# Block-causal attention with a top-1 MoE: x rows fetched four slots ahead, and the router of one batch laid beside its ranks

## Chip, core and metric

One Trainium2 chip, one core of it. The time is device microseconds (us) of one launch, from the first to the last instruction and what the launch has around it. Three runs of the kernel before gave 879.25, 882.23 and 882.85 us, so the median is 882.23 us.

The engines are named as in the profile: PE multiplies matrices (PEld loads its weights), DVE, ACT and POOL work on tiles, SP issues most of the loads. An engine executes its instructions strictly in the order in which they stand in its program. A name with q behind it (SPq) is the engine's own instruction queue: loads that it issues, branches, register loads.

## The reference

q, k, v are 8 batches x 8 heads x 576 tokens x 64. The attention is block-causal (blocks of 64 tokens); its output, 4608 tokens x 512, goes into a mixture of 8 experts of which each token takes one.

```python
scores = np.matmul(q, k.transpose(0, 1, 3, 2)) / 8
scores = np.where(pos[:, None] // 64 >= pos[None, :] // 64, scores, -1e9)
attn = softmax(scores)
x = np.matmul(attn, v).transpose(0, 2, 1, 3).reshape(4608, 512)

logits = normed(x) @ normed(expert_emb).T / tau        # 4608 x 8
expert = argmax(logits, axis=1)
gate = softmax(logits)[expert]
for e in range(8):
    m = expert == e
    out[m] = gate[m, None] * (relu(x[m] @ w1[e]) @ w2[e])   # 512 -> 1024 -> 512
```

## The kernel before, in words

**Attention (0 to about 341 us).** The work is cut in 32 pairs of heads, and each pair in pieces (scores, maxes, values and sums, finish) that a hand-written string orders. The router of a batch, `route(b)`, is a generator that gives one step at a time to places in those strings: the highest logit of a token, its expert, its rank among the tokens of that expert (`above`, `places`), the norm of its row (`squares`, then a power on POOL), the gate (`gx`, an exp on ACT), and at last five scatters (L654, an indirect DMA from POOL) that write the rows of x, with the gate and the token's number behind each row, into a DRAM buffer `xs` sorted by expert. Batch 6 (`b == B - 2`) is the last batch but one, and its router also decides which rows of two "early" tiles are valid (`einv`, `lack`).

**Early tiles (about 344 to 384 us).** Two tiles of 128 rows of expert 0 are calculated before the other tokens are sorted, with the chain that makes the tables of slots running beside them. Their rows are loaded by `early_rows` (`ex`, `eg`), and `place` makes from the token numbers the indices `ei` of the rows of the output.

**Slots (about 384 us to the end).** Up to 43 slots of 128 sorted rows, 36 of which run. Per slot: the first layer `ph` (PE, three products for each pair of tiles, since each fp32 operand is split in a high and a low part), relu on ACT to `h`, 16 transposes of `h` on DVE to `pt`, the split of `pt` into `hh` (ACT) and `hl` (DVE), the second layer `py` (PE), the scaling by the gate (ACT, `y`), the indirect store (POOL). `back(g)` writes down the engines' work in a fixed order; PE gets the second layer of slot g-1 behind the first layer of slot g. The rows of x are loaded into `xq` (four DMAs of 64 KB) and `gt` (gate and token) by `fetch(g)`, transposed on DVE to `px` (`xturn`), and split on ACT and POOL.

**Weights.** An expert has a ring half of `ring_h` and `ring_l` for each layer. At the first slot of an expert, ACT makes `ring_h` from `raw` (eight casts), POOL makes `ring_l = raw - ring_h` (eight subtractions), and SP loads the next expert's `raw` in four DMAs of 512 KB for each layer. "raw0" is the first layer's weights, "raw1" the second's. All this is conditional (`tc.If`, L1005 on SP) on a flag of the slot, read into registers on ACT, POOL and SP (`flags`, L968 and L969).

**SP's order.** In a steady slot SP has: the register loads of `flags`, the If of raw1, the If of raw0, `fetch` (a register load of the place, then `xq` x4 and `gt`), and so again. For 3 <= g < 8 `fetch` also has a `clear`: 260 KB of zeros written behind the last rows of an expert in `xs`, and the load of x waits for it to land. `fetch(3)` stands behind slot 0's `give_slot`.

Of the kernel before, what the change touches and what calls it, by code (L numbers as in the profile page):

```python
# [48 lines left out]
def kernel(  # L49
# [515 lines left out]
    def route(b, xrow, lgh, ssp):  # L565
# [3 lines left out]
        t1 = sm.tile([P, NJ, E], F32, name="t1")  # L569
        ohb, acc = hot[b % 2][:, 0:NJ, :], hot[b % 2][:, NJ, :]  # L570
        eng = nc.gpsimd if b < B - 1 else nc.vector
        nc.vector.tensor_reduce(lg, lgh.rearrange("p j h e -> p j e h"), axis=AX.X, op=ALU.add)
        yield
        nc.vector.tensor_reduce(mx, lg, axis=AX.X, op=ALU.max)
        yield
        eng.tensor_tensor(lg, lg, bc(mx.unsqueeze(2), P, NJ, E), op=ALU.subtract)
        yield

        nc.vector.scalar_tensor_tensor(t1, lg, 0.0, erev, op0=ALU.is_ge, op1=ALU.mult)
        yield  # L580
        nc.vector.tensor_reduce(mx, t1, axis=AX.X, op=ALU.max)
        yield
        nc.vector.tensor_tensor(ohb, t1, bc(mx.unsqueeze(2), P, NJ, E), op=ALU.is_equal)
        yield
        nc.vector.memset(ohb[64:P, NJ - 1, :], 0.0)
        yield
# [10 lines left out]
        if b < B - 1:  # L597
            t2 = above(rk)
            give_bank(rb)
        yield  # L600
        acc = hot[(b + 1) % 2][:, NJ, :]
        with nc.allow_low_precision(reason="whole numbers up to 42"):
            nc.vector.tensor_reduce(acc, hot[b % 2].rearrange("p j e -> p e j"), axis=AX.X, op=ALU.add)
        yield
# [6 lines left out]
        if b == B - 2:  # L611

# [6 lines left out]
            give_bank(cb)  # L619
            yield  # L620
            nc.vector.tensor_scalar(lack, miss, 0.0, float(EARLY), op0=ALU.max, op1=ALU.min)
            nc.gpsimd.tensor_scalar(einv, lim2, miss, BIG, op0=ALU.is_le, op1=ALU.mult)
            yield
            nc.vector.tensor_tensor(acc[:, 0:1], acc[:, 0:1], lack, op=ALU.add)
            yield

        ss = sm.tile([P, NJ], F32, name="ss")
        gs = sm.tile([P, NJ], F32, name="gs")
        if b < B - 1:
            for j in range(NJ):  # L630
                squares(xrow[:, j, 0:DM], ss[:, j:j + 1])
                yield
        else:
            nc.vector.tensor_reduce(ss, ssp, axis=AX.X, op=ALU.add)
        nc.gpsimd.tensor_tensor(ss, ss, half, op=ALU.pow)
        if b == B - 1:
            yield
        eng.tensor_scalar(ss, ss, 1.0e-6, None, op0=ALU.add)
        yield
        if b < B - 1:  # L640
            rowj = yield from places(t2, ohb, nc.gpsimd)
            yield
        nc.vector.reciprocal(ss, ss)
        yield
        eng.tensor_tensor(lg, lg, bc(ss.unsqueeze(2), P, NJ, E), op=ALU.mult)
        yield
        nc.scalar.activation(gx[b % 2][:, :, 0:E], lg, AF.Exp)
        yield
        nc.vector.tensor_reduce(gs, gx[b % 2], axis=AX.X, op=ALU.add)
        yield  # L650
        nc.vector.reciprocal(xrow[:, :, DM:DM + 1], gs.unsqueeze(2))
        yield
# [8 lines left out]
        if b == B - 2:  # L661
            slow.append(early_rows())
# [15 lines left out]
    def early_rows():  # L678
# [3 lines left out]
        for u in range(EARLY):  # L682
            place(ei[:, u:u + 1], eg[u], einv[:, u:u + 1])
# [177 lines left out]
    def counts():  # L861
# [26 lines left out]
        for e in range(AHEAD):  # L888
            clear(e)
        yield  # L890

# [48 lines left out]
    AHEAD = 3  # L940
    NFIRST = 5

# [65 lines left out]
    def fetch(g):  # L1008
        xq, gt = take("xq"), take("gt")
        if AHEAD <= g < E:  # L1010
            clear(g)
# [119 lines left out]
    def chain():  # L1131
# [18 lines left out]
        for u in range(60):  # L1150
            for w in list(work):
                try:
# [3 lines left out]
                    if w is tw:  # L1156
                        work.append(slot_places(0, NFIRST))
# [8 lines left out]
        for g in range(AHEAD):  # L1166
# [48 lines left out]
    rotate(mp, "gt", 5, [P, 2], F32)  # L1215
# [27 lines left out]
    def l2(g, parts):  # L1243
# [3 lines left out]
        if NF - 1 in parts:  # L1247
            u = g - NSLOT
# [209 lines left out]
```

## Time and profile before

| | |
|---|---|
| median of three runs | 882.23 us (879.25 to 882.85) |
| profiled execution, its own time | 879.04 us |
| its span, first to last instruction | 877.3 us |
| PE busy | 774.6 us (88% of the span) |
| DVE, POOL, ACT busy | 612.6, 461.1, 409.8 us |
| granted clock of PE, mean | 0.956 of full speed |
| 344.65 to 384.15, early tiles | PE busy 28.95 of 39.50 us |
| 384.15 to 455.58, slots 0 to 2 | PE busy 50.37 of 71.43 us |
| 455.58 to 655.92, slots on to the last stall | PE busy 155.67 of 200.34 us |
| 655.92 to the end | PE busy 209.81 of 221.41 us |

PE is the busiest engine; its idle time lies almost wholly between 341 and 656 us. A row of a timeline gives the start in us, the length, engine, line, operation, the tiles written and read, how many instructions are merged in the row, and in square brackets the engine's idle time just before it and what ended that idle time. "[11.02 <-ACT hh L1107]" says that the engine stood 11.02 us and went on when ACT had written hh in line 1107.

### The profile page before, as it was taken

What the parts mean: (1) busy time and instruction counts of PE and PEld (TensorE: products, weight loads), DVE (VectorE), ACT (ScalarE), POOL (GpSimd) and SP (SyncE); (2) the same over time, 40 slices, a digit from 0 to 9 for tenths busy, and PEclk for the clock granted to TensorE, in tenths of its full rate; (3) what the DMA queues carried; (4) which work ended last, traced back from release to release, by engine and by line L of the source; (5) the groups of instructions that cost most, each with busy time, mean ns of one, the idle gap of its engine ahead of it and who ended that gap; (6) DMA issues with size and microseconds to landing.
All of it is one profiled execution on the core that took longest, in us unless ns stands there. A gap on an engine that the chain in (4) does not pass through costs nothing. (4 is left out here: it accounts for less than half of the span.)

```text
span 877.3 us, 23684 instructions
## 1 busy us (share of the span) xinstructions
PE 774.6 (88%) x6989; PEld 619.4 (71%) x6989; DVE 612.6 (70%) x1363; ACT 409.8 (47%) x831; POOL 461.1 (53%) x462
## 2 busy tenths in 40 slices
PE   8999999999999997688489864968959999999994
PEld 3788878887888776466368653857838888888873
DVE  6577778777877775663778653747837888888870
ACT  2566666767676674354243361514423333443321
POOL 6556757686777765432534574646643222572221
PEclk9999999999999999899889978888979999999998
DMA  5645576563745403858254545454153111111110
GB/s 124 145 111 116 135 121 158 115 147 82 175 104 118 130 3 93 219 179 246 63 143 155 116 130 127 133 133 134 50 147 121 50 51 51 38 54 54 50 48 21
DMA packets 164234, 96.29 MB, mean 110 GB/s; under 512 B 125709, under 2 KB 146509, under 8 KB 164060
## 3 DMA queue, kind: packets, MB, share of 16 engines
q1 hardware_dynamic: 157084, 72.67, 35.6%
q0 software_dynamic: 6976, 21.66, 6.8%
q8 instruction: 65, 1.06, 0.5%
q14 instruction: 109, 0.89, 0.4%
HBM read 72.44 MB, written 23.27 MB: 109 GB/s over the span
## 5 line engine op out<-in xcount | busy, mean ns | idle before, releaser
L1101 DVE STREAM_TRANSPOSE pt<-h 32x256 f32<-32x256 f32 x528 | 240.7, 456 | 40.2 <-ACT h L1075 22.9
L1048 PE MATMUL py<-ring_h,hh 128*128 x272 | 113.7, 418 | 60.1 <-ACT hh L1107 60.0
L849 POOL TENSOR_TENSOR ring_l<-raw,ring_h 128x1024 f32 (+1 forms) x49 | 116.7, 2413 | 42.5 <-ACT ring_h L844 38.3
L361 DVE TENSOR_REDUCE nmx<-psm 128x16 f32<-128x1024 f32 (+2 forms) x128 | 125.6, 986 | 13.8 <-PE psm L355 10.9
L1048 PE MATMUL py<-ring_l,hh 128*128 x272 | 112.0, 412 | 0.0
L1048 PEld LDWEIGHTS py<-ring_h,hh 128*128 128x128 f32 x272 | 54.3, 200 | 75.9 <-ACT hh L1107 62.5
L844 ACT CAST ring_h<-raw 128x1024 f32 (+1 forms) x62 | 60.9, 1047 | 82.5 <-SPq L1005 63.8
L397 POOL TENSOR_TENSOR pS<-pS,pT 128x640 f32<-128x640 f32 (+2 forms) x93 | 93.5, 1006 | 9.8 <-ACT pT L423 4.1
L423 ACT ACTIVATE pT<-psm 128x640 f32<-128x640 f32 (+2 forms) x128 | 89.2, 703 | 18.5 <-PE psm L355 12.2
L1028 POOL TENSOR_TENSOR xl<-px,xh 128x512 fp32r<-128x512 f32 x34 | 43.8, 1289 | 98.3 <-ACT tb L958 75.4
L1048 PE MATMUL py<-ring_h,hl 128*128 x272 | 91.8, 400 | 0.0
L1048 PE MATMUL ph<-ring_h,xh 128*128 x280 | 87.4, 393 | 3.7 <-ACT y L1114 1.5
L1048 PE MATMUL ph<-ring_l,xh 128*128 x280 | 86.8, 391 | 0.4 <-POOLq L998 0.4
L1115 POOL DMA_INDIRECT out_dram<-y,oi x36 | 38.1, 1058 | 83.4 <-POOLq L998 34.9
L451 PE MATMUL psm<-pT,vo 128*64 128x320 f32 (+2 forms) x640 | 75.9, 380 | 0.0
L1114 ACT ACTIVATE y<-py,gt 128x512 f32<-128x512 f32 x34 | 23.4, 688 | 99.0 <-PE py L1048 97.1
L1048 PE MATMUL ph<-ring_h,xl 128*128 x280 | 69.1, 389 | 0.0
L416 PE MATMUL psm<-qh,kh 64*128 64x320 f32 (+4 forms) x384 | 66.8, 341 | 0.6 <-DVE ql L339 0.3
L1107 ACT CAST hh<-pt 128x512 fp32r<-128x512 f32 x66 | 35.5, 589 | 65.0 <-DVE pt L1101 63.9
L1048 PEld LDWEIGHTS ph<-ring_h,xh 128*128 128x128 f32 x280 | 52.3, 188 | 16.5 <-ACT y L1114 2.0
L1048 PEld LDWEIGHTS py<-ring_l,hh 128*128 128x128 f32 x272 | 54.3, 200 | 13.1
L451 PEld LDWEIGHTS psm<-pT,vo 128*64 128x64 f32 x640 | 43.2, 137 | 28.2 <-ACT pT L423 0.4
(260 smaller groups left out, 1674.1 us busy)
## 6 DMA issues: line engine op xcount, KB each, us to landing
raw<-in_moe_w_dram SPq DMA_DIRECT2D x60, 512.0 KB
xq<-xs SPq DMA_DIRECT2D x152, 64.0 KB
qn<-in_q_dram SPq DMA_DIRECT2D x64, 128.0 KB
kn<-in_k_dram SPq DMA_DIRECT2D x64, 128.0 KB
vo<-in_v_dram SPq DMA_DIRECT2D x64, 128.0 KB
xs<-zcol SPq DMA_DIRECT2D x8, 260.0 KB
raw<-in_moe_w_dram POOLq DMA_DIRECT2D x4, 512.0 KB, 4.6
qa<-nmT SPq DMA_DIRECT2D x64, 2.5 KB
```

What stands on the lines that cost most here:

```text
L361: nc.vector.tensor_reduce(m[:, :, f:f + o // w], mt[:, :, 0:o].rearrange("p h (b c) -> p h b c", c=w), axis=AX.X, op=ALU.max, negate=True)
L397: nc.gpsimd.tensor_tensor(o, o, pT[:, :, off[t]:off[t] + w], op=ALU.add)
L416: nc.tensor.matmul(st[0:kw, hh, o:o + c1 - c0], kk[hd[hh], t * P:t * P + kw], qq[hd[hh], 64 + c0:64 + c1], start=(x == 0), stop=(x == len( ...
L423: nc.scalar.activation(pT[:, :, f:f + w] if c0 else pA, st[:, :, 0:w], AF.Exp, scale=scale)
L451: m = nc.tensor.matmul(ob[hh * D:(hh + 1) * D, b0:b0 + q1 - c0], rows(vo, ends_v, n, t)[:, hh, :], pTs[hh][0][:, f0:f0 + q1 - c0] if c0 el ...
L844: return (nc.scalar.copy if eng is nc.scalar else eng.tensor_copy)(piece(ring_h, to, c, half), raw[i][:, c * CW:(c + 1) * CW])
L849: return eng.tensor_tensor(piece(ring_l, to, c, half), raw[i][:, c * CW:(c + 1) * CW], piece(ring_h, to, c, half).bitcast(F32), op=ALU.sub ...
L1028: eng.tensor_tensor(xl, slots[g]["px"].rearrange("p (c t) -> p c t", t=P), xh.bitcast(F32), op=ALU.subtract)
L1048: m = nc.tensor.matmul(out, ac, slots[g]["w", i](r, c * n + off), start=(u == 0 and c == 0), stop=(c == nk - 1 and u == len(turns) - 1))
L1101: nc.vector.transpose(pt[32 * j:32 * j + 32, :, 32 * i:32 * i + 32], h[32 * i:32 * i + 32, :, j, :])
L1107: nc.scalar.copy(sets["hh"][u], pt[:, 4 * u:4 * u + 4])
L1115: nc.gpsimd.indirect_dma_start(out=out, out_offset=bass.IndirectOffsetOnAxis(ap=to, axis=0), in_=y, in_offset=None, bounds_check=NT - 1, o ...
```

## The change

Three things are altered. First, `fetch` runs four slots ahead instead of three (`AHEAD`), and stands at the start of `back(g)`, not at its end. The three unconditional fetches and clears ahead of the slots stay three (`CLEAR`); `fetch(3)`, with its clear, goes between the loads of raw1 and raw0 in the early part, `fetch(4)` takes its old place, and `fetch(5)` is the first thing of `back(1)`. `gt` gets seven buffers. The tables' first piece covers eight slots (`NPLACE`) instead of five. Second, in `route(6)` the squares, the power and the gate are given out beside the rank's steps and not behind them, and `einv` and `lack` are made after the scatters. Third, the indices `ei` are made in `l2`, at the end of an early tile, and no longer in `early_rows`.

```diff
@@ route(b): the pieces, as generators
+        def gate_beside():
+            yield from norm_at_once()
+            power()
+            yield
+            yield
+            bump()
+            yield
+            yield from gate()
+        beside = gate_beside() if b == B - 2 else None
+        def also():
+            if beside is not None:
+                next(beside, None)
         nc.vector.tensor_reduce(mx, lg, axis=AX.X, op=ALU.max)
+        also()
         yield
...
         if b == B - 2:
-            nc.vector.tensor_scalar(lack, miss, 0.0, float(EARLY), op0=ALU.max, op1=ALU.min)
-            nc.gpsimd.tensor_scalar(einv, lim2, miss, BIG, op0=ALU.is_le, op1=ALU.mult)
-            yield
-            nc.vector.tensor_tensor(acc[:, 0:1], acc[:, 0:1], lack, op=ALU.add)
-            yield
...
         for j in range(NJ):
             w = nc.gpsimd.indirect_dma_start(
...
         if b == B - 2:
+            nc.vector.tensor_scalar(lack, miss, 0.0, float(EARLY), op0=ALU.max, op1=ALU.min)
+            nc.gpsimd.tensor_scalar(einv, lim2, miss, BIG, op0=ALU.is_le, op1=ALU.mult)
+            yield
+            nc.vector.tensor_tensor(acc[:, 0:1], acc[:, 0:1], lack, op=ALU.add)
             slow.append(early_rows())
@@ early_rows
             load_x(ex[u], eg[u], slice(u, u + 1))
             yield
-        for u in range(EARLY):
-            place(ei[:, u:u + 1], eg[u], einv[:, u:u + 1])
@@
-    AHEAD = 3
+    AHEAD = 4
     NFIRST = 5
+    NPLACE = 8
@@ fetch
-        if AHEAD <= g < E:
+        if CLEAR <= g < E:
             clear(g)
@@ l2
             u = g - NSLOT
+            place(ei[:, u:u + 1], eg[u], einv[:, u:u + 1])
             give(g, slots[g]["py"], eg[u][:, 0:1], ei[:, u:u + 1])
@@
     load_raw(1, 1)
+    fetch(3)
     slots[0]["w", 0] = half_of(0, 0)
@@ back(g)
         byT = g in TURNED
+        if g + AHEAD < NSLOT:
+            fetch(g + AHEAD)
         if g + 1 < NSLOT:
...
         if g == FLAGS_AT:
             slot_flags(NFIRST, NSLOT)
-            for _ in slot_places(NFIRST, NSLOT):
+            for _ in slot_places(NPLACE, NSLOT):
                 pass
-        if g + AHEAD < NSLOT:
-            fetch(g + AHEAD)
         next_low(g, 1, (0, 1))
```

SP at the start of slot 1, before: the flags of slots 1 and 2 are read (`tb`), and the If of the first layer's weights follows at once.

```order
L968 TENSOR_LOAD tb_6348
L968 ISA x2
L969 TENSOR_LOAD tb_6348
L969 ISA x2
L1005 COMPARE_AND_BRANCH
L164 ISA
L164 DMA raw_124<-in_moe_w_dram 32x4x1024
```

SP at the same place after: a clear and the load of slot 5's x stand between the flags and the If (L1058 is the old L1005; four like loads of `xq` and one of `gt`).

```order
L1022 TENSOR_LOAD tb_6348
L1022 ISA x2
L945 TENSOR_LOAD zrow
L945 ISA x2
L946 ISA
L946 DMA xs<-zcol 128x520
L1065 TENSOR_LOAD tix
L1065 ISA x2
L723 ISA
L723 DMA xq_6334<-xs 32x4x128
```

What moved: a whole `fetch` with its clear is now ahead of the If that loads raw0.

POOL around the scatters of batch 6, before: sums of the last pairs' exponentials (`pS`, from which PE makes the denominators), the norm and gate of the tokens (`ss`, `lg`), five scatters, the early indices (`ei`).

```order
L635 TENSOR_TENSOR ss<-ss,half 128x5
L638 TENSOR_SCALAR ss<-ss 128x5
L694 TENSOR_TENSOR t_5918<-t_5918,hot_107 128x40
L397 TENSOR_TENSOR pS<-pS,pT_211 128x2x192
L397 TENSOR_TENSOR pS<-pS,pT_211 128x2x64
L645 TENSOR_TENSOR lg<-lg,ss 128x40
L654 DMA xs<-xrow,rowj 37888x520 x5
L676 TENSOR_SCALAR ei<-exg_218,einv 128x1
L676 TENSOR_SCALAR ei<-exg_219,einv 128x1
L844 CAST ring_h_6212<-raw_124 128x1024 x2
```

POOL at the same place after:

```order
L591 TENSOR_TENSOR lg<-lg,ss 128x40
L397 TENSOR_TENSOR pS<-pS,pT_211 128x2x320
L767 MEMSET xrow 128x5x8
L768 COPY xrow<-toki 128x5
L702 DMA xs<-xrow,rowj 37888x520 x5
L711 TENSOR_SCALAR einv<-lim_103,miss 128x2
L397 TENSOR_TENSOR pS<-pS,pT_211 128x2x192
L397 TENSOR_TENSOR pS<-pS,pT_211 128x2x64
L894 CAST ring_h_6210<-raw_124 128x1024 x2
L168 DMA raw_6212<-in_moe_w_dram 128x2x512 x4
```

What moved: the gate is made earlier, the two last sums stand behind the five scatters and not ahead of them, and the early indices no longer stand between the scatters and the load of raw1.

SP in a steady slot, before: the loads of raw0 and of x wait, in turn, for the same four of SP's eight DMA semaphores (DMAHW; a load that uses one again waits until the load that used it last has landed).

```order
L164 DMA raw_124<-in_moe_w_dram 32x4x1024 [waits DMAHW0_49]
L164 ISA
L164 DMA raw_124<-in_moe_w_dram 32x4x1024 [waits DMAHW1_49]
L1005 UNCONDITIONAL_BRANCH
L1005 UNCONDITIONAL_BRANCH [waits DMAHW0_49,DMAHW1_49,DMAHW6_49,DMAHW7_49]
L1012 TENSOR_LOAD tix
L1012 ISA x2
L671 ISA
L671 DMA xq_6337<-xs 32x4x128 [waits DMAHW6_49,DVE_49]
```

SP in a steady slot, after (buffers of x two slots later than before, every other row in the order that it had):

```order
L164 DMA raw_124<-in_moe_w_dram 32x4x1024 [waits DMAHW6_49]
L164 ISA
L164 DMA raw_124<-in_moe_w_dram 32x4x1024 [waits DMAHW7_49]
L1058 UNCONDITIONAL_BRANCH
L1058 UNCONDITIONAL_BRANCH [waits DMAHW4_49,DMAHW5_49,DMAHW6_49,DMAHW7_49]
L1065 TENSOR_LOAD tix [waits DVE_49]
L1065 ISA x2
L723 ISA
L723 DMA xq_6333<-xs 32x4x128 [waits DMAHW4_49,DVE_49]
L723 ISA
L723 DMA xq_6333<-xs 32x4x128 [waits DMAHW5_49]
```

What moved: nothing but the slot whose x is loaded; `fetch` follows the If of raw0 as it did, since the end of `back(g)` and the start of `back(g + 1)` are the same place for SP.

## Rows read from the trace of the kernel before

**Rows 1.** Waits from 425 to 700 us: in total, times, longest.

```profile
PE py L1048 <- ACT hh L1107: 60.0, 6, 13.7
...
ACT ring_h L844 <- SPq L1005: 59.7, 6, 14.9
...
DVE px L1018 <- DMA xq<-xs: 44.1, 6, 12.0
```

**Rows 2.** Timeline of PE: the stalls' ends, start, length, idle time before.

```profile
441.35 0.80 PE L1048 MATMUL py<-ring_h,hh 128*128 x1 [13.74 <-ACT hh L1107]
...
455.58 0.51 PE L1048 MATMUL py<-ring_h,hh 128*128 x1 [1.56 <-ACT hh L1107]
...
511.28 0.79 PE L1048 MATMUL py<-ring_h,hh 128*128 x1 [11.02 <-ACT hh L1107]
```

**Rows 3.** Timeline of ACT: casts of weights and splits of pt.

```profile
424.11 3.89 ACT L844 CAST ring_h<-raw 128x1024 f32 x4 [2.31 <-SPq L1005]
...
440.71 1.07 ACT L1107 CAST hh<-pt 128x512 fp32r<-128x512 f32 x2 [12.13 <-DVE pt L1101]
...
453.05 1.99 ACT L844 CAST ring_h<-raw 128x1024 f32 x2 [3.77 <-SPq L1005]
...
508.75 1.99 ACT L844 CAST ring_h<-raw 128x1024 f32 x2 [13.24 <-SPq L1005]
```

**Rows 4.** Timeline of SP in the same stalls: loads of raw and x, clears.

```profile
492.73 1.90 SPq L164 DMA_DIRECT2D raw<-in_moe_w_dram  x4
498.22 7.86 SPq L671 DMA_DIRECT2D xq<-xs  x4
```

**Rows 5.** Timeline of DVE: transposes of x.

```profile
420.44 0.71 DVE L1018 STREAM_TRANSPOSE px<-xq 128x512 f32<-128x512 f32 x1 [7.02 <-DMA xq<-xs]
...
508.24 0.71 DVE L1018 STREAM_TRANSPOSE px<-xq 128x512 f32<-128x512 f32 x1 [9.83 <-DMA xq<-xs]
```

**Rows 6.** Timeline of SP from slot 0's end to slot 2's loads.

```profile
402.84 1.48 SPq L894 DMA_DIRECT2D xs<-zcol  x1
...
416.70 1.90 SPq L671 DMA_DIRECT2D xq<-xs  x4
...
425.00 0.39 SPq L894 DMA_DIRECT2D xs<-zcol  x1
...
429.24 0.35 SPq L673 DMA_DIRECT2D gt<-xs  x1
...
435.18 1.88 SPq L164 DMA_DIRECT2D raw<-in_moe_w_dram  x4
```

**Rows 7.** Timeline of POOL: slot 2's low parts.

```profile
425.30 9.85 POOL L849 TENSOR_TENSOR ring_l<-raw,ring_h 128x1024 f32 x4 [2.14 <-ACT ring_h L844]
```

**Rows 8.** Windows: us, busy (instructions) of PE, PEld, DVE, ACT, POOL; clock, DMA share, GB/s.

```profile
441.35:448.39 7.04, 7.04 (x24) 5.65 (x25) 6.20 (x14) 1.99 (x5) 1.57 (x2) 0.79 0.84 218
455.58:461.29 5.71, 5.71 (x25) 4.61 (x25) 4.94 (x11) 3.85 (x7) 5.29 (x4) 1.00 0.34 89
```

**Rows 9.** Timeline of POOL: last sums, scatters of batch 6, early indices, raw1's load, casts.

```profile
328.15 1.54 POOL L397 TENSOR_TENSOR pS<-pS,pT 128x384 f32<-128x384 f32 x2
...
330.92 1.11 POOL L654 DMA_INDIRECT xs<-xrow,rowj  x1 [1.02 <-DVE rin L528]
...
336.17 0.97 POOL L654 DMA_INDIRECT xs<-xrow,rowj  x1 [0.30 <-issue]
...
343.50 0.31 POOL L676 TENSOR_SCALAR ei<-exg,einv 128x1 int32<-128x1 int32 x1 [6.35 <-DMA exg<-xs]
...
348.19 3.02 POOL L168 DMA_DIRECT2D raw<-in_moe_w_dram  x4
...
364.10 1.04 POOL L844 CAST ring_h<-raw 128x1024 fp32r<-128x1024 f32 x1 [3.87 <-DMA raw<-in_moe_w_dram]
```

**Rows 10.** Timeline of PE from the last attention sums to the early tiles' second layer.

```profile
344.65 0.50 PE L1048 MATMUL psm<-ring_h,xh 128*128 128x512 f32 x1 [3.89 <-ACT xh L1024]
...
368.24 0.80 PE L1048 MATMUL psm<-ring_l,hh 128*128 128x512 f32 x1 [5.37 <-DVE ring_l L849]
```

More of the change, by code (lines that the diff above doesn't have):

```diff
@@ L599, in route @@
             give_bank(rb)
+        also()
         yield
@@ L603, in route @@
             nc.vector.tensor_reduce(acc, hot[b % 2].rearrange("p j e -> p e j"), axis=AX.X, op=ALU.add)
+        also()
         yield
@@ L611, in route @@
         if b == B - 2:
+            pl = places(t2, ohb, nc.gpsimd)
+            next(pl)
             cb = take_bank()
@@ L619, in route @@
             give_bank(cb)
+            also()
             yield
-            nc.vector.tensor_scalar(lack, miss, 0.0, float(EARLY), op0=ALU.max, op1=ALU.min)
-            nc.gpsimd.tensor_scalar(einv, lim2, miss, BIG, op0=ALU.is_le, op1=ALU.mult)
+            next(pl)
+            also()
             yield
-            nc.vector.tensor_tensor(acc[:, 0:1], acc[:, 0:1], lack, op=ALU.add)
+            next(pl)
+            also()
             yield
[L627 to L631, printed above, removed]
+            try:
+                next(pl)
+            except StopIteration as e:
+                rowj = e.value
+            for _ in beside:
                 yield
[L633 to L636, printed above, removed]
+        elif b < B - 2:
+            yield from norm_at_once()
+            power()
+            bump()
             yield
-        eng.tensor_scalar(ss, ss, 1.0e-6, None, op0=ALU.add)
-        yield
-        if b < B - 1:
             rowj = yield from places(t2, ohb, nc.gpsimd)
             yield
-        nc.vector.reciprocal(ss, ss)
-        yield
[L645 to L652, printed above, removed]
+            yield from gate()
+        else:
+            power()
+            yield
+            bump()
+            yield
+            yield from gate()
         for j in range(NJ):
@@ L661, in route @@
         if b == B - 2:
+            nc.vector.tensor_scalar(lack, miss, 0.0, float(EARLY), op0=ALU.max, op1=ALU.min)
+            nc.gpsimd.tensor_scalar(einv, lim2, miss, BIG, op0=ALU.is_le, op1=ALU.mult)
+            yield
+            nc.vector.tensor_tensor(acc[:, 0:1], acc[:, 0:1], lack, op=ALU.add)
             slow.append(early_rows())
@@ L887, in counts @@
         nc.vector.scalar_tensor_tensor(zrow, kbase, float(P), cnt, op0=ALU.mult, op1=ALU.add)
-        for e in range(AHEAD):
+        for e in range(CLEAR):
             clear(e)
         yield
+    CLEAR = 3
     def clear(e):
@@ L1156, in chain @@
                     if w is tw:
-                        work.append(slot_places(0, NFIRST))
+                        work.append(slot_places(0, NPLACE))
                         tw = None
@@ L1165, in chain @@
         slot_flags(0, NFIRST)
-        for g in range(AHEAD):
+        for g in range(CLEAR):
             fetch(g)
@@ L1214 @@
     rotate(mp, "xq", 4, [P, QD, P], F32)
-    rotate(mp, "gt", 5, [P, 2], F32)
+    rotate(mp, "gt", 7, [P, 2], F32)
     rotate(mp, "oi", 2, [P, 1], I32)
```

28 lines of the change are left out of this document (added).

## The prediction

> **What bounds the kernel now.** I read the busy shares first, then PE's waits, then the timelines of the engines that PE waits for. PE is the bound: what doesn't move a PE gap doesn't count. From 425 to 700 us PE lost 60.0 us in six waits for ACT's `hh` [rows 1]. Beside them stand two more totals of six waits each: ACT's casts waited 59.7 us for SP to pass an If, and DVE waited 44.1 us for x [rows 1]. The change goes at the 44.1. So the question is which of the two ends last in each stall.
>
> In the stall that ends at 511.28 (11.02 us, [rows 2]) the answer stands in three timelines. SP issues the loads of raw0 at 492.73; the four loads of x that follow take SP 7.86 us, from 498.22 to 506.08 [rows 4], though a free load of x is issued in 1.90 us (the one at 416.70, [rows 6]). The order on SP says why: loads reuse eight semaphores in turn, and the four of x get those that the four loads of raw0 have just taken, so SP stands until each 512 KB has landed. Only then does SP come to the flags and the next If. ACT's casts of raw1 may not go before SP has passed this If: they start at 508.75 after 13.24 us [rows 3]; `hh` stands behind them on ACT, and PE starts at 511.28. DVE's x comes at 508.24 after 9.83 us [rows 5]. DVE and ACT are let go within 0.5 us of each other, since both waited for the same landing.
>
> **x earlier, in a steady slot.** The fetch moves from the end of one `back` to the start of the next but for two slots later. For SP these are one place: raw0's If, fetch, flags, raw1's If, as before, and the semaphore rows behind the If are as before. So x is there in time and DVE's waits go, but SP still stands 7.9 us on raw0's landing, ACT's casts still wait for the If (59.7 us in all), and `hh` still stands behind them. The four stalls at or behind 511.28 are 60.0 - 13.74 - 1.56 = 44.7 us [rows 1, 2]. I take their change as 0. Bounds: if ACT didn't wait too, all would go (-44.7); a loss isn't excluded, since the loads of x now stand two slots ahead of need, but they are as many as before, of 0.26 MB a slot.
>
> A rule of the Trainium skill speaks against the change at this place, and the rest can do without it. The row shows SP's 7.86 us ahead of the loads [rows 4]. "DMA: Bandwidth & Descriptors", section "Anatomy of one DMA", says that DMA engines don't wait on semaphores: each wait is the issuing sequencer's, ahead of the dispatch. The trace agrees: what waits here is SP, with all behind it, and not a transfer. If the wait were a queue's, the If would pass at once and the sum would be some 40 us lower.
>
> **The first stall, ending at 441.35 (13.74 us), and slots 1 to 3.** Here DVE was the late one: it waited 7.02 us for x at 420.44, then wrote the tables of slots, then did 16 transposes of `h`, and `hh` waited 12.13 us for these [rows 3, 5]. With x there, DVE is up to 7.0 us earlier. But SP gets more to do ahead of slot 1's If on raw0, which lets ACT's four casts go at 424.11 [rows 3]:
> - `fetch(3)` with its clear now goes ahead of raw0's early load, which comes later by its issues, some 2.5 to 3.5 us (five issues at about 0.5 us each, 1.90 us for the four of x, [rows 6]). The next clear lands behind these weights, as the one at 402.84 did: its x was issued at 416.70, 13.9 us later [rows 6]. I take +3.2 us (2 to 4.5).
> - `fetch(5)`, with a clear, is new ahead of that If. The same thing in the trace lies between the If (424.0, by ACT's start) and the end of the load of `gt`, 429.24 + 0.35 = 429.6 [rows 3, 6]: +5.6 us (lower bound 3.5, if the clear lands at once; upper 14, if it lands as the one at 402.84).
>
> So the If is passed at 424.0 + 3.2 + 5.6 = 432.8. The casts take 3.89 us and `hh` goes behind them, at about 437; PE starts at about 438, 3.3 us earlier than 441.35. That is all of DVE's 7.0 that remains. And it isn't kept: POOL's four subtractions start behind the casts and take 9.85 us, their end (435.15) lets SP load slot 3's raw0 at 435.18 [rows 6, 7], and this load's landing is what SP waits for before it passes the If at 453.05 that ended the small stall at 455.58 [rows 2, 3]. Each of these stands 8.8 us later now. From 455.58 to the next stall PE has hardly a gap, so nothing buys this back: **+8.7 us** at 455.58. PE then stands some 12 us there and not 1.56, so it starts at a lower clock. The work behind a stall took 7.04 us at a granted clock of 0.79, the like without a stall 5.71 us at 1.00 [rows 8]: **+1.3 us**; the stall at 438 keeps its own.
>
> **Norm and gate beside the ranks; the early indices.** The number of operations stays: 5 squares, a power, the gate, five scatters. What moves is POOL's order. The scatters ran from 330.92 to 337.14, 6.2 us [rows 9], behind the last sums `pS` of attention; now the last two sums, which PE needs for a pair's denominators, stand behind the scatters. The scatters' places (ranks) set their start, not the gate, so they stay at about 331. The two sums ended at 328.15 + 1.54 = 329.69 [rows 9]; behind the scatters they end at 337.14 + 1.54 = 338.7, 9.0 us later. Attention ends about as much later, and of this PE's gap before the early tiles (3.89 us, [rows 10]) takes about 3: the tiles start +6.0 us later, at about 350.7. Against that: the early indices waited 6.35 us for their rows [rows 9], with POOL's load of raw1 behind them (348.19, [rows 9]). This load no longer waits so; POOL's casts that waited for it until 364.10 [rows 9], and PE's 5.37 us behind them [rows 10], get closer. By these rows the start of the slots moves by 6.0 - 5.37 - about 2 = **-1.2 us**, and I keep -4 to +6 (the upper end if the loads land as before).
>
> **Sum.** 8.7 + 1.3 - 1.2 = +8.8 us. The profiled execution took 879.04 us, 1.74 around its span of 877.3; with 8.8 more it is 887.8. The median before, 882.23, is 3.2 above the profiled one, so the prediction is 882.23 + 8.8 = **891 us**.
>
> **Rivals.**
> - *The whole change comes to nothing* (within half a per cent, 877.8 to 886.6, about what a measurement of this kernel can tell from no change). SP's extra steps cost 3.5 + 2 and not 8.8, as the clear lands at once, and the transition gives 1 to 4 back: 882.2 + 5.4 - 3 = 884.6. For it: the chance that the loads are later by less, since the bounds of the two clears are wide. Chance 0.21.
> - *The tail of attention isn't bought back.* raw1 lands as late as before, and the 6.0 us remain: 882.2 + 10 + 6 - 2 = 896. For it: PE's sums behind the scatters are sure, the earlier landing is not. Chance 0.12.
> - *The first stall decides, faster.* DVE's 7.02 us at 420.44 are won, and slot 1's If is not the later: if the clears of slots 3 to 5 land within 2 us and the casts go by 426, POOL's chain moves by under 3 us, and the gap of 1.56 us takes part of it. Then 882.2 - 7.0 + 0 - 1.2 = 874. It decides once SP passes the If before about 426. Against it: five more issues, two register loads and a clear stand there. Chance 0.11.
> - *x is what binds*, faster: ACT's wait for SP is a symptom of DVE's, and all six waits for x become PE time. 44.7 of stalls go but for about 1.2 each, and four restarts at 1.3: 882.2 - 40 - 5 + 8.8 = 846. Against it: SP's row of 7.86 us, which is older than DVE's need. Chance 0.06.
> - *The change doesn't do what it says*: the loads of x "ahead of the weights' loads" still stand behind the weights' loads of the slot before. That is part of my forecast, and not a case of its own.
>
> **How the numbers follow.** My forecast, slower, 886.6 to 895: 0.50; the cases above 0.21, 0.12, 0.11, 0.06. Slower by over 0.5%: 0.50 + 0.12 = 0.62; within: 0.21; faster: 0.17. The range: I leave out x-binds (0.06), half of the first-stall case, and the far ends of the tail case: 875 to 899.
>
> **What would show it.** Right: DVE's wait for `xq` falls from 44.1 us to under 10, and PE's wait for `hh` stays at 44 or more behind 500 us, with the loads of x on SP still taking 7 us or more, and ACT's casts released by the If; the PE start that was 455.58 comes 5 to 10 us later, with over 8 us idle before it; the first stall ends earlier by 2 to 5 us against the start of the slots. PE's last sums of attention come behind POOL's scatters. Wrong: if the four stalls shrink below 5 us each (then x bound), or the start at 455.58 comes no later against the slots' start (then SP's added steps are covered).

## The result, and the profile after

The changed kernel takes 887.55 us (median of eight runs, 884.56 to 890.06); the kernel before, in eight runs beside them, 879.38 us (878.45 to 882.85). The ratio (of the means) is 1.0085 with a 95% interval of 1.0061 to 1.0109: 7.5 us slower, between 5.4 and 9.6; the medians are 8.2 apart. The prediction was 891 us, 8.8 us slower, with a range of 875 to 899; it stood on a median of three runs of the kernel before, which was 2.9 us above that of eight. The profiled execution took 885.97 us, 1.7 us around its span of 884.3; that of before 879.04 and 877.3.

Nearly all of the difference is there at the second stall, and little comes behind it. PE's timeline of the changed kernel has these starts (start, length, instruction, idle time before it and what ended it; L1101 is the old L1048, L1160 the old L1107), to be held against [rows 2, 10].

```profile
350.57 0.51 PE L1101 MATMUL psm<-ring_h,xh 128*128 128x512 f32 x1 [1.80 <-ACT xh L1077]
...
382.47 0.50 PE L1101 MATMUL psm<-ring_h,xh 128*128 128x512 f32 x1 [3.11 <-ACT xh L1077]
...
437.58 0.80 PE L1101 MATMUL py<-ring_h,hh 128*128 x1 [12.40 <-ACT hh L1160]
...
462.10 0.79 PE L1101 MATMUL py<-ring_h,hh 128*128 x1 [11.48 <-ACT hh L1160]
...
518.63 0.79 PE L1101 MATMUL py<-ring_h,hh 128*128 x1 [10.59 <-ACT hh L1160]
...
658.29 0.80 PE L1101 MATMUL py<-ring_h,hh 128*128 x1 [10.52 <-ACT hh L1160]
```

| PE start | before | after | difference |
|---|---|---|---|
| early tiles | 344.65 | 350.57 | +5.9 |
| slots | 384.15 | 382.47 | -1.7 |
| end of the first stall | 441.35 | 437.58 | -3.8 |
| next start behind `hh` | 455.58 | 462.10 | +6.5 |
| first stall behind 500 us | 511.28 | 518.63 | +7.35 |
| span | 877.3 | 884.3 | +7.0 |

The waits from 425 to 720 us, to be held against [rows 1] (engine, what waited, for what: us in total, times, longest):

```profile
ACT ring_h L894 <- SPq L1058: 82.7, 6, 16.5
...
PE py L1101 <- ACT hh L1160: 67.8, 6, 12.6
```

DVE's 44.1 us of waits for x are gone: the list has no such row any more. PE's wait for `hh` is not smaller but larger, 67.8 us against 60.0, and ACT's for SP rose from 59.7 to 82.7. The last four stalls are 67.8 - 12.40 - 11.48 = 43.9 us, as against 44.7.

SP's timeline shows both halves of the forecast. In the stall that ends at 518.63 the four loads of x still take SP 8.10 us behind those of raw0, as 7.86 in [rows 4]; their x is now for two slots later. In the early slots it has two more fetches ahead of the load of raw0 at 442.61, which was at 435.18 in [rows 6].

```profile
389.46 0.37 SPq L946 DMA_DIRECT2D xs<-zcol  x1
395.81 3.32 SPq L723 DMA_DIRECT2D xq<-xs  x4
...
404.76 2.42 SPq L946 DMA_DIRECT2D xs<-zcol  x1
418.74 1.90 SPq L723 DMA_DIRECT2D xq<-xs  x4
...
424.83 0.38 SPq L946 DMA_DIRECT2D xs<-zcol  x1
426.98 1.92 SPq L723 DMA_DIRECT2D xq<-xs  x4
429.09 0.35 SPq L725 DMA_DIRECT2D gt<-xs  x1
...
442.61 1.89 SPq L164 DMA_DIRECT2D raw<-in_moe_w_dram  x4
...
500.38 1.89 SPq L164 DMA_DIRECT2D raw<-in_moe_w_dram  x4
505.44 8.10 SPq L723 DMA_DIRECT2D xq<-xs  x4
```

A clear that stands alone lets the load of x go 2.15 us later (424.83 to 426.98); the one at 389.46, issued 2.9 us behind the start of 2 MB of weights, 6.35 us later; the one at 404.76, behind 4 MB, 14.0 us later. The Trainium skill, "DMA: Bandwidth & Descriptors", section "Anatomy of one DMA", gives some 2 us as the fixed part of a transfer, most of it the receipt of the write, for DMAs that GpSimd issues; the lone clear, issued by SP and with its 260 KB counted in, is of that size, and the last one took six and a half times as long with the weights ahead of it.

ACT tells what the two stalls cost. Its four casts went at 432.06 and not at 424.11 [rows 3], and the next pair at 459.57 and not at 453.05:

```profile
432.06 3.88 ACT L894 CAST ring_h<-raw 128x1024 f32 x4 [16.48 <-SPq L1058]
...
436.94 1.07 ACT L1160 CAST hh<-pt 128x512 fp32r<-128x512 f32 x2 [0.41 <-ACTq L1039]
...
459.57 1.99 ACT L894 CAST ring_h<-raw 128x1024 f32 x2 [13.69 <-SPq L1058]
```

DVE had its 16 transposes ready at 427.0 (its row is below), ten us ahead of `hh`, which in the kernel before had waited for them. So the first stall changed its cause: it was DVE's, and is now that of SP, through ACT.

```profile
419.20 7.80 DVE L1154 STREAM_TRANSPOSE pt<-h 32x256 f32<-32x256 f32 x16
...
438.05 1.29 DVE L1162 TENSOR_TENSOR hl<-pt,hh 128x512 fp32r<-128x512 f32 x2 [10.30 <-ACT hh L1160]
```

### The profile page after: what moved, and what is told of

It reads as the page before. It is cut to its first block, busy times and chain, and to the rows that moved or that the text cites. A ratio compares the mean times of both kernels' runs of the same rounds, so it can differ in the third digit from the quotient of the medians.

```text
span 884.3 us, 23732 instructions
## 1 busy us (share of the span) xinstructions
PE 778.5 (88%) x6989; PEld 624.3 (71%) x6989; DVE 606.4 (69%) x1363; ACT 409.8 (46%) x831; POOL 463.7 (52%) x462
## 5 line engine op out<-in xcount | busy, mean ns | idle before, releaser
L1101 PE MATMUL py<-ring_h,hh 128*128 x272 | 115.3, 424 | 67.9 <-ACT hh L1160 67.8
L1101 PEld LDWEIGHTS py<-ring_h,hh 128*128 128x128 f32 x272 | 55.0, 202 | 83.7 <-ACT hh L1160 70.3
L1101 PE MATMUL py<-ring_l,hh 128*128 x272 | 113.6, 418 | 0.0
L1162 DVE TENSOR_TENSOR hl<-pt,hh 128x512 fp32r<-128x512 f32 x66 | 42.5, 686 | 89.9 <-ACT hh L1160 89.9
L1101 PE MATMUL py<-ring_h,hl 128*128 x272 | 91.8, 400 | 0.0
L1101 PE MATMUL ph<-ring_h,xh 128*128 x280 | 86.8, 391 | 2.4 <-ACT y L1167 1.5
L1101 PE MATMUL ph<-ring_l,xh 128*128 x280 | 86.4, 390 | 0.4 <-POOLq L1051 0.4
L1101 PE MATMUL ph<-ring_h,xl 128*128 x280 | 69.2, 389 | 0.0
L1101 PEld LDWEIGHTS py<-ring_l,hh 128*128 128x128 f32 x272 | 55.2, 203 | 13.1
L1101 PEld LDWEIGHTS ph<-ring_h,xh 128*128 128x128 f32 x280 | 52.6, 188 | 14.2 <-ACT y L1167 2.0
```

The source lines that it names most:

```text
L1101: m = nc.tensor.matmul(out, ac, slots[g]["w", i](r, c * n + off), start=(u == 0 and c == 0), stop=(c == nk - 1 and u == len(turns) - 1))
L1162: nc.vector.tensor_tensor(sets["hl"][u], pt[:, 4 * u:4 * u + 4], sets["hh"][u].bitcast(F32), op=ALU.subtract)
```

## The experiments

They ran on three chips, on each of which the kernel before takes 897 to 899 us: `router_only`, `fetch_only`, `raw0_behind_raw1` and `x_behind_raw1` on chip 1; `late_catch_up`, `clears_first`, `raw0_by_pool` and `after_x_behind_raw1` on chip 4; the others on chip 3. On chip 3, which has a trace of the kernel before (the last experiment), it is slower ahead of the slots, and from the slots' start to the end it takes as long as on the first chip. All ratios are to runs of the kernel before on the same chip; times read from traces of different chips are compared only from the slots' start, unless the text says otherwise.

### The change in two halves

`router_only` has the router's part and the early indices, with the fetch of before:

```diff
-    AHEAD = 4
-    NPLACE = 8
+    AHEAD = 3
...
     load_raw(1, 1)
-    fetch(3)
...
-        if g + AHEAD < NSLOT:
-            fetch(g + AHEAD)
         if g + 1 < NSLOT:
...
+        if g + AHEAD < NSLOT:
+            fetch(g + AHEAD)
         next_low(g, 1, (0, 1))
```

> Only the second and third part of the change (norm and gate of batch 6 beside its ranks; early indices in the early tiles' second layer); the fetch as before. The change as a sum of parts: early tiles start at about 350.6, the slots 1.7 us earlier than before, PE's idle time before slot 2's second layer again under 3 us, time 876 to 879, that is 1 to 2 us faster than before. Rival (the parts act on each other: the slots' start gains only with the new fetch): slots start 3 us or more later than before, 882 to 885.

Measured: 897.71 us against 897.73, ratio 0.9998 (0.9981 to 1.0016). The stalls are those of the kernel before.

`fetch_only` is the other half, the same lines the other way round, put into the kernel before.

> Only the first part of the change (x four slots ahead, fetch(3) and fetch(5) with their clears ahead of raw0's loads of slots 0 and 1, tables in a piece of eight); the router as before. Sum of parts: the first stall ends about 3 us earlier, the next start of PE has 10 to 13 us idle before it and comes 7 to 9 us later than 455.58, the four stalls stay; 886 to 890. Rival (the loss comes from the router's part): 876 to 881.

Measured: ratio 1.0101 (1.0078 to 1.0123), 907.95 us. The slots start at 404.08, and PE's second start with a stall has 11.17 us idle before it, 82.0 us behind the slots' start; in the kernel before it is 71.4 (455.58 - 384.15). PE in the kernel with the fetch alone:

```profile
404.08 0.50 PE L1051 MATMUL psm<-ring_h,xh 128*128 128x512 f32 x1 [3.01 <-ACT xh L1027]
...
486.10 0.79 PE L1051 MATMUL py<-ring_h,hh 128*128 x1 [11.17 <-ACT hh L1110]
```

So all of the loss is the fetch's (its interval and that of the whole change, 1.0061 to 1.0109, overlap). The first stall did not come 3 us earlier against the slots' start here (57.15 us behind it, as before), so that part of what I expected missed. The router's part is worth nothing that can be measured; the 1 to 2 us I expected from it missed as well.

### Where in the fetch's part the loss lies

`late_catch_up` is the changed kernel, but with the places of before for slots 3 to 10; from slot 8 on x is four slots ahead:

```diff
     load_raw(1, 1)
-    fetch(3)
...
-    fetch(AHEAD)
+    fetch(3)
...
-        if g + AHEAD < NSLOT:
+        if g == E:
+            fetch(g + 3)
+        if g >= E and g + AHEAD < NSLOT:
             fetch(g + AHEAD)
...
+        if g < E:
+            fetch(g + 3)
         next_low(g, 1, (0, 1))
```

> The changed kernel, but slots 3 to 10 are fetched at the places of the kernel before (fetch(3) behind slot 0's store, then slot g + 3 at the end of back(g)); from slot 8 on x is four slots ahead as in the changed kernel, by one fetch more there. Theory (the loss is SP's added steps ahead of raw0's loads in slots 0 and 1; x early in later slots neither gains nor loses): the second stall of the changed kernel (11.5 us idle) falls to under 3 us, the last three stalls stay at 10 to 12 us although DVE no longer waits for x there, ratio to the kernel before 0.996 to 1.003. Rival (x two slots earlier costs in every slot): ratio over 1.005. Rival x (late x binds): the last three stalls fall to under 5 us, ratio under 0.975.

Measured: ratio 0.9960 (0.9938 to 0.9983), 896.20 us. The second stall is gone (no idle time over 1 us between 461.67 and 530), and the loss with it: 1.25% less than the changed kernel. In the last three stalls x is early, and they are as long as ever (12.53, 9.71 and 10.88 us idle). Waits of this kernel from 500 to 720 us:

```profile
ACT ring_h L894 <- SPq L1058: 52.9, 4, 15.3
...
PE py L1101 <- ACT hh L1160: 43.6, 4, 12.5
...
DVE px L1071 <- DMA xq<-xs: 9.0, 1, 9.0
```

DVE waited once (at 527.11, in the first of these four stalls), and PE four times, 43.6 us in all. So x ahead of need neither costs nor gains in a later slot, and the loss is in the first ones. This kernel keeps the longer first piece of the tables and the seven buffers of `gt`, so the loss isn't theirs.

`clears_first` is the changed kernel with the clears of all eight experts where the first three stood, and none in a fetch:

```diff
-    CLEAR = 3
+    CLEAR = E
...
-        for g in range(CLEAR):
+        for g in range(3):
             fetch(g)
```

> The changed kernel, but all eight clears stand with the first three, when the tables are made, and no fetch has a clear. Theory (SP's added steps, the wait for a clear's landing most of all): SP passes slot 1's If on raw0 10 us or more earlier against the slots' start, the second stall falls to under 6 us, ratio to the kernel before 0.988 to 1.001. Rival (the five loads of x and their register steps are the cost, not the clears): second stall stays over 8 us, ratio over 1.004.

Measured: ratio 0.9960 (0.9942 to 0.9977). PE's first two stalls in it:

```profile
449.84 0.79 PE L1101 MATMUL py<-ring_h,hh 128*128 x1 [2.57 <-ACT hh L1160]
...
469.74 0.79 PE L1101 MATMUL py<-ring_h,hh 128*128 x1 [7.07 <-ACT hh L1160]
```

They fell from 12.4 and 11.5 to 2.6 and 7.1 us, and SP passes slot 1's If 12.4 us earlier against the slots' start (ACT's casts at 441.75 - 404.56 = 37.2 us, in the changed kernel at 432.06 - 382.47 = 49.6). The second stayed just over the 6 us I had set. Against the slots' start the second of them ends after 65.2 us (469.74 - 404.56), where the changed kernel needs 79.6 and the kernel before 71.4. Of SP's added steps the clears, with the waits for their landing, are thus the larger part, and without them the four-slot fetch is no longer slower than the kernel before.

### What holds the four later stalls

The theory: SP stands behind raw0's landing, and ACT may not cast before SP has passed the next If. Moving either the fetch or the load of raw0 on SP, and nothing else, tells it from the theory that x is late, and from the one that the load and POOL's subtractions themselves are the bound.

`raw0_behind_raw1`, the kernel before with raw0's If moved behind the next slot's If of raw1:

```diff
         next_low(g - 1, 1, (2, 3))
+        if g > 1:
+            next_load(g, 0)
...
-        if NPC - 1 in cs:
-            with tc.If(sl["first_sp"] != 0):
-                load_raw(i, sl["en2"])
+        if NPC - 1 in cs and (i == 1 or g == 1):
+            next_load(g, i)
+
+    def next_load(g, i):
...
+        with tc.If(sl["first_sp"] != 0):
+            load_raw(i, sl["en2"])
```

> The kernel before, with one thing moved: a slot's conditional load of raw0 stands on SP behind the next slot's conditional load of raw1, and so behind the fetch of x, not ahead of both. Theory SP (ACT's casts are held because SP stands on raw0's landing before it comes to the If of raw1): the four stalls behind 500 us (44.7 us) fall to under 3 us each, ACT's waits for SP's If to under 15 us in all, and the time falls by 30 to 48 us, to about 840. DVE's waits for x go too, since x is no longer behind raw0. Rival (the stall is the 9.5 us of POOL's subtractions and raw0's bandwidth, whoever waits): the stalls stay over 8 us each, under 10 us gained.

Measured: ratio 0.9803 (0.9778 to 0.9827), some 17.7 us faster. Three of the four stalls are small, one is not. PE in this kernel:

```profile
550.39 0.79 PE L1054 MATMUL py<-ring_h,hh 128*128 x1 [10.91 <-ACT hh L1113]
...
594.69 0.80 PE L1054 MATMUL py<-ring_h,hh 128*128 x1 [3.16 <-ACT hh L1113]
```

The one that is left has the same mechanism with the layers changed round: raw0's If now stands on SP behind raw1's, whose last load was issued at 540.6, and ACT's casts of raw0 waited for SP to pass it, as ACT's timeline says:

```profile
544.87 1.99 ACT L844 CAST ring_h<-raw 128x1024 f32 x2 [16.41 <-SPq L1011]
```

The direction was right, and the size was half of what I expected. ACT's waits for SP fell only to 44.6 us and not under 15, and DVE still waited 12.8 us for loads of x between 440 and 740 us. From the slots' start to the end this kernel takes 475.7 us, against 491.8 in the last experiment's trace of the kernel before. PE's waits for `hh` fell by 33.7 us (58.1 to 24.4), but its other idle time rose by 12.9 us and its busy time by 4.8 (417.0 to 421.8).

`x_behind_raw1`, the kernel before with one statement moved:

```diff
         next_low(g - 1, 1, (2, 3))
+        if g + AHEAD < NSLOT:
+            fetch(g + AHEAD)
         next_high(g + 1, 0, range(NPC))
...
-        if g + AHEAD < NSLOT:
-            fetch(g + AHEAD)
         next_low(g, 1, (0, 1))
```

> The kernel before, with the fetch of slot g + 3 moved from the end of back(g) to a place between the conditional loads of raw1 and raw0, so that x is ahead of raw0's load and the If of raw1 is the next thing behind it. Theory SP: DVE's wait for x falls from 44 us to under 10, but SP now stands in the not-taken side of raw1's If, which waits for the same four semaphores as raw0's loads; ACT's casts still wait for it, the four stalls stay at 8 to 12 us each, and the time is 868 to 884. Rival x (the late x is what binds): all four stalls go, time 835 to 850.

Measured: ratio 0.9762 (0.9733 to 0.9790), some 21.4 us faster, and so between the two. My own expectation missed by its size, and DVE's waits for x fell to 16.4 us and not under 10: the stalls behind 500 us are 6.77, 3.66, 8.40 and 1.07 us. The timeline of ACT in the second of these shows why:

```profile
556.88 1.05 ACT L844 CAST ring_h<-raw 128x1024 f32 x1 [3.72 <-SPq L1005]
559.99 1.04 ACT L844 CAST ring_h<-raw 128x1024 f32 x1 [2.06 <-SPq L1005]
560.94 1.06 ACT L1107 CAST hh<-pt 128x512 fp32r<-128x512 f32 x2
```

SP does stand in the side of raw1's If that isn't taken, as I thought. But from there it let ACT's two casts go one by one: they went at 556.88 and 559.99, 4.9 and 8.0 us after raw0's issue at 551.95. My reading is that SP gives its four semaphores on one by one, as the quarters of raw0 land, and that each cast needs one of them; no row shows the quarters' landing. In the kernel before, SP had all four landings, the load of `gt` and the flags' registers to get through first, and the casts went 16.0 us after raw0's issue (492.73 to 508.75, [rows 3, 4]), and 15.3 to 15.9 us in the other three stalls. The two longer stalls here, 6.77 and 8.40 us, have both casts together, 12.4 us after raw0's issue (517.95 to 530.39 and 591.85 to 604.27): that is earlier than before, but not one by one, and what sets these two apart isn't shown.

SP's timeline of this kernel has raw0's issue:

```profile
551.95 1.96 SPq L164 DMA_DIRECT2D raw<-in_moe_w_dram  x4
```

`after_x_behind_raw1` makes the same move in the changed kernel:

> The changed kernel, with the fetch of slot g + 4 moved behind the conditional load of raw1, ahead of that of raw0. If the place on SP is what gains (SP has fewer steps behind raw0's landing before ACT may go) and the slots ahead are not: stalls behind 500 us as with x behind raw1 at three slots ahead (1 to 8.5 us each, 22 in all), second stall as in the changed kernel or somewhat less; ratio 0.976 to 0.986. If four slots ahead gives more: ratio under 0.972.

Measured: ratio 0.9760 (0.9727 to 0.9793), the same as with three slots ahead. This is the cleanest test of SP's order: x is early in the changed kernel and here alike (between 425 and 720 us DVE waits for no load of x in either), and only the place of the fetch on SP differs. PE's waits for `hh` behind 500 us are 13.9 us, where the changed kernel has 43.9 and I had expected 22. ACT's casts go 15.2 to 15.7 us after raw0's issue in the changed kernel (500.38 to 516.11 in the stall shown above); here they go one by one, 5.1 to 8.1 us after it, in three stalls, and both together after 12.4 us in the fourth. PE's waits from 500 to 720 us, then ACT in the first of these stalls (raw0 was issued at 514.35):

```profile
PE py L1101 <- ACT hh L1160: 13.9, 5, 8.2
```

```profile
519.45 1.05 ACT L894 CAST ring_h<-raw 128x1024 f32 x1 [2.17 <-SPq L1058]
...
521.91 1.04 ACT L894 CAST ring_h<-raw 128x1024 f32 x1 [1.42 <-SPq L1058]
```

So what counts behind 500 us is what stands on SP between raw0's load and the If that ACT waits for. That the ratio is the same as with three slots ahead doesn't make the number of slots worth nothing: behind 500 us PE waits 13.9 us for `hh` here and 20.4 there, but ahead of 500 us 19.1 here (12.89 and 6.26) and 8.3 there. What four slots gain behind 500 us they lose ahead of it.

`raw0_by_pool`, the kernel before with raw0's load issued by POOL, in the If of its own last subtraction:

```diff
+        sl["en2_pool"] = nc.values_load(tb[0:1, 2:3], min_val=0, max_val=E - 1, engines=[ET.Pool])
...
                 ins = split_lo(i, c, 1 - sl["pd", "pool"], eng=nc.gpsimd)
+                if i == 0 and c == NPC - 1:
+                    load_raw(0, sl["en2_pool"], eng=nc.gpsimd)
...
-        if NPC - 1 in cs:
+        if NPC - 1 in cs and i == 1:
             with tc.If(sl["first_sp"] != 0):
```

> The kernel before, with the conditional load of raw0 issued by POOL behind its own last subtraction, and not by SP. Theory SP: SP has no If of raw0 and nothing on it waits for raw0's landing; DVE's waits for x and ACT's waits for SP go to under 15 us in all, the four stalls fall to under 5 us each, unless POOL's own stores wait for raw0's landing (up to 6 us a time); ratio 0.950 to 0.980. Rival (the four stalls are raw0's traffic and POOL's subtractions): stalls stay over 8 us, ratio over 0.99.

Measured: ratio 1.0105 (1.0072 to 1.0138), slower; the expected gain did not come. PE's waits for `hh` are gone but for the first stall, which bears the theory out, and the wait went to POOL with the load: ACT's casts now wait for POOL's Ifs, and PE for POOL's part of x (`xl`). The rows that name raw0's landing for POOL itself come to 13.6 and 3.7 us; how much of POOL's 37.7 us behind its own stores is raw0's isn't shown. Waits from 440 to 740 us:

```profile
ACT ring_h L844 <- POOLq L999: 40.2, 6, 11.7
POOL oi L676 <- DMA out_dram<-y,oi: 37.7, 9, 6.0
...
PE ph L1051 <- POOL xl L1031: 23.9, 7, 6.1
...
PE py L1051 <- ACT hh L1110: 15.8, 1, 15.8
...
POOL oi L676 <- DMA raw<-in_moe_w_dram: 13.6, 2, 6.8
```

### Both findings together

`clears_first_x_behind_raw1` joins the two edits above in the changed kernel.

> The changed kernel with both later findings: all clears stand when the tables are made, and the fetch of slot g + 4 is behind the conditional load of raw1. If the two gains add, as they should when they lie in different slots: the first two stalls as with the clears first (2.6 and 7 us, not 12.9 and 6.3), those behind 500 us as with x behind raw1, ratio to the kernel before 0.960 to 0.970. If they are the same gain twice: 0.974 to 0.980.

Measured: ratio 0.9700 (0.9660 to 0.9740), 871.35 us against 896.99: the fastest, faster than both kernels, at the edge of what I expected from a plain sum (0.960 to 0.970). The first stalls are 2.58 and 5.92 us. The eight clears cost something earlier: PE waited 6.19 us at the start of the slots, where the kernel before on this chip waited 2.99.

`three_ahead_clears_first` makes them in the kernel before, so x is three slots ahead and the router as it was.

> The kernel before (router as it was, x three slots ahead) with all clears first and the fetch behind the conditional load of raw1. If four slots ahead, fetch(3) early and the router's part are worth nothing by themselves: the same as the changed kernel with these two moves, ratio 0.960 to 0.972. If x three slots ahead comes late once more: DVE waits over 15 us for x between 425 and 720 us, ratio over 0.975.

Measured: ratio 0.9810 (0.9763 to 0.9856). That is no faster than without the clears moved (0.9762), and slower than with four slots ahead, against the first of the two cases that I had set. The second doesn't hold as I set it either: DVE waits 3.7 us for x in all, and not over 15. Its first stall is 12.86 us, where the four-slot kernel has 2.58: `hh` waited 11.58 us there for DVE's transposes, and DVE had waited 3.73 us for x and then spent 13 us on the tables (6 in the changed kernel). So the earlier x does have a worth, in the first slots, once the clears don't take it back. Not all of it stays: counted from the slots' start, PE ends the first stall behind 500 us after 121.1 us here (528.53 - 407.41) and after 113.4 with four slots ahead (518.65 - 405.29), and of these 7.8 us 3.2 are left at the end (469.5 and 466.3 us). Another 2.1 us lie in the slots' start itself, 407.41 and 405.29, each in one profile. I have no run that parts the router's half from it here.

`clears_first_raw0_behind_raw1` has the other way of freeing SP:

> The changed kernel with all clears first and, in place of the moved fetch, the conditional load of raw0 moved behind that of the next slot's raw1. Theory SP: as with raw0 behind raw1 alone (stalls behind 500 us under 4 us but for an expert of few slots, where ACT waits for SP to pass raw0's If behind raw1's landing, 8 to 11 us), and the gain of the clears on top; ratio 0.965 to 0.975.

Measured: 0.9797 (0.9731 to 0.9862), with one stall of 12.28 us left at 540.84, which I take for the case of an expert with few slots. The interval is wide and doesn't tell it from raw0 behind raw1 alone (0.9803).

`before_again` is the kernel before, unchanged.

> The kernel before, unchanged, for a trace from the same chip as the other runs: start of the slots at 403 to 408 us, stalls as in its first trace (13.7, 1.6, then four of 10 to 12.5 us). If the router's part moves the slots' start by 1 to 2 us, as the two first traces have it, this start is 1 to 2 us behind that of the kernel with the router's part alone (402.7).

Measured: 895.95 us in one run. PE's start of the early tiles and of the slots, in the kernel before on chip 3 and then with the router's part alone on chip 1:

```profile
362.26 0.50 PE L1048 MATMUL psm<-ring_h,xh 128*128 128x512 f32 x1 [1.83 <-ACT xh L1024]
...
402.44 0.50 PE L1048 MATMUL psm<-ring_h,xh 128*128 128x512 f32 x1 [2.99 <-ACT xh L1024]
```

```profile
370.63 0.50 PE L1098 MATMUL psm<-ring_h,xh 128*128 128x512 f32 x1 [1.80 <-ACT xh L1074]
...
402.69 0.50 PE L1098 MATMUL psm<-ring_h,xh 128*128 128x512 f32 x1 [1.70 <-ACT xh L1074]
```

Between these two the early tiles come 8.4 us later and are 8.1 us shorter, and the slots start at the same time; on the first chip it was 5.9 and 7.6 us. But the two traces are of different chips. On chip 1 two kernels have the code of the kernel before up to the slots: `raw0_behind_raw1` starts the early tiles at 367.08 and the slots at 406.08, `x_behind_raw1` at 366.61 and 409.48. Held against these, the router's part would let the slots start 3.4 to 6.8 us earlier. Single profiles ahead of the slots thus differ by more than the 1 to 2 us in question, and what decides is the ratio of 0.9998 over 12 and 17 runs on one chip: no gain and no loss that can be told from none. From the slots' start to the end the kernel before takes 894.2 - 402.4 = 491.8 us here and 493.2 on the first chip.

## Why the prediction was right, step by step

- **The four later stalls stay** (taken as 0): right, 43.9 us against 44.7. DVE's waits went to nothing and PE got none of it. The reason given, that SP stands on raw0's landing and ACT on SP, is shown by runs that change one of the two: with x early and SP as it was, the last stalls stay (`late_catch_up`); with x as early and only SP's order changed, they fall from 43.9 to 13.9 us (`after_x_behind_raw1` against the changed kernel). `x_behind_raw1` and `raw0_behind_raw1` agree, but there x comes earlier too.
- **fetch(3) with its clear early, +3.2 us**: the load of x behind the next clear went at 418.74 and not 416.70, 2.0 us later on the clock and 3.7 us against the slots' start.
- **fetch(5) ahead of the If, +5.6 us**: from that load to ACT's casts it is 13.3 us (418.74 to 432.06), before it was 7.4 (416.70 to 424.11): +5.9 us.
- **The first stall, 3.3 us earlier; the next start, 8.7 us later with some 12 us idle**: 3.8 us earlier on the clock, 2.1 against the slots' start; then 8.2 us later against the slots' start, with 11.48 us idle. The If was passed at 432.06 (432.8 was forecast), and PE started at 437.58 (438). DVE was in fact ready 13.6 us earlier and not 7.0 (its transposes end at 427.0, before at 440.6), since its work on the tables was shorter as well; it didn't matter, as SP was the later. `late_catch_up` and `clears_first` show that the place and the clears are the cause.
- **The restart at a lower clock, +1.3 us**: the 7.04 us behind 462.10 ran at a granted clock of 0.78, as the mechanism has it, and the 5.71 us behind 455.58 in the kernel before at 1.00 [rows 8]. Yet from there to the last stall's end both kernels need the same but for 0.3 us (462.10 to 658.29 is 196.2, and 455.58 to 651.46 is 195.9), since the four stalls are 0.8 us shorter. So the sum was 1 us too high here, though less for the restart itself than for stalls taken as unchanged.

```profile
462.10:469.14 7.04, 7.04 (x24) 5.64 (x25) 6.20 (x13) 3.99 (x7) 6.88 (x4) 0.78 0.46 122
```

- **The router's part, -1.2 us**: -1.7 on the first chip, in one profile each, and nothing in the ratio of `router_only`; by its size no run bears it out. The order of events was as forecast: PE's sums of attention started behind POOL's scatters, at 337.77 behind `pS`; the early tiles came 5.9 us later (6.0 was forecast); and the tiles got shorter, as POOL's load of raw1 went at 345.53 and not at 348.19. PE and POOL of the changed kernel:

```profile
337.77 0.30 PE L470 MATMUL psm<-pS,ones 128*32 128x128 f32 x1 [2.58 <-POOL pS L397]
```

```profile
335.27 0.97 POOL L702 DMA_INDIRECT xs<-xrow,rowj  x1 [0.30 <-issue]
336.33 0.32 POOL L711 TENSOR_SCALAR einv<-lim,miss 128x2 f32<-128x2 f32 x1
336.73 1.52 POOL L397 TENSOR_TENSOR pS<-pS,pT 128x384 f32<-128x384 f32 x2
...
345.53 3.02 POOL L168 DMA_DIRECT2D raw<-in_moe_w_dram  x4
```

- **Sum**: +8.8 forecast, +7.5 measured. Two terms were rounded loosely (3.2 + 5.6 is 8.8, not 8.7, and 6.0 - 5.37 - 2 is -1.4, not -1.2), which changes nothing. Of the rivals, "x is what binds" fell by `late_catch_up`, and "the first stall decides" by the changed kernel's own ACT row at 432.06: SP passed the If well behind the 426 that it had set.
- **What the prediction didn't see**: half of the 44.7 us could be had by one statement's place. In the expectation of `x_behind_raw1` I took the If itself for as bad a place to stand in as the loads of x, and it isn't: with SP there, ACT's casts went 4.9 to 12.4 us after raw0's issue, and not 15.3 to 16.0.

## What to carry to other kernels

When two engines wait behind the same landing, read which instruction of the issuing queue each of them is released by, not which transfer it needs: taking away one of the two waits gave nothing here. Before a transfer is moved earlier, count what the queue then has to do ahead of the next transfer on the critical path, above all a wait for a write to land behind megabytes of loads. In a queue that executes in order, look for the place where the least stands between a long transfer's issue and the branch or signal that others wait for; here that was worth 2.4%, and 3% with x four slots ahead and the clears out of the way.

## What the runs showed of the hardware that was not expected

- Small DVE instructions took several times as long while POOL worked. The last table instructions before slot 1's transposes (128 x 38 and 128 x 35 elements) ran in the kernel before while POOL subtracted (425.30 to 435.15, [rows 7]), and in the changed kernel ahead of POOL's subtractions:

```profile
426.85 1.46 DVE L912 SCALAR_TENSOR_TENSOR tix<-gi,top,tq 128x38 int32<-128x38 f32 x1
428.23 2.38 DVE L914 SCALAR_TENSOR_TENSOR tq<-gi,tq 128x38 f32<-128x38 f32 x1
430.64 2.25 DVE L916 TENSOR_SCALAR inv<-tq,pcol 128x38 f32<-128x38 f32 x1
```

```profile
418.65 0.26 DVE L964 SCALAR_TENSOR_TENSOR tix<-gi,top,tq 128x35 int32<-128x35 f32 x1
...
419.05 0.24 DVE L968 TENSOR_SCALAR inv<-tq,pcol 128x35 f32<-128x35 f32 x1
```

  The first fence is of the kernel before, the second of the changed one: 6.1 us for three against 0.7 (the one left out took 0.19). The kernel with three slots ahead and the clears first shows the slow form again (2.38, 2.38 and 2.25 us), again with POOL's subtractions beside it. In the kernel before each of the three ended within 0.1 us of the end of one of POOL's subtractions (428.31, 430.61 and 432.89 against 428.25, 430.55 and 432.85), as if it had stood until POOL was through. One and the same table instruction, on 1 x 304 elements, took 1.47 us at 422.02 in the kernel before, where POOL worked from 421.88 to 423.16 (L1028), and 0.46 us at 413.96 in the changed one, where POOL stood idle. That POOL is the cause is argued from this overlap, and no run took POOL's work away by itself. The Trainium skill, "GPSIMD Engine Reference", section "Architecture", says that POOL's physical ports are shared with DVE, which the rows agree with; that section gives no size.
- The same program took 879 us on the first chip and 897 to 899 on chips 1, 3 and 4. On chip 3 the whole difference lies ahead of the slots (362.26 against 344.65 at the early tiles). Its cause is open.
